# A three-layer kernel with a retention stage: one TensorE visit per retention unit, and the state product taken with a block-diagonal 128x128 operand

## The chip, the cores and the metric

The program runs on one core of one Trainium2 chip. The metric is the device time of one execution in microseconds (us). The core has TensorE (PE in the profile; PEld is its weight load), VectorE (DVE), ScalarE (ACT), GpSimd (POOL) and SyncE (SP), which here issues the DMAs. Each of them works through its own list of instructions in order.

## The reference, cut to what matters

```python
scores = scale * q @ k.T                       # 8 batches, 8 heads, 576 positions, 64 features, all float32
rel = pos[:, None] - pos[None, :]
Dmat = np.where(rel >= 0, gamma[head] ** rel, 0.0)
att = (scores * Dmat) @ v                      # retention
x = att, heads side by side                    # 4608 tokens x 512
h = x @ w_in;  y = (h * cos(h)) @ w_out        # 512 -> 2048 -> 512
z = max(y @ w1, y @ w2, y @ w3) @ w_out2       # 512 -> 768 -> 512
```

gamma is one constant below 1 for each head. The three dense layers make up most of the work; the change touches only the retention, the second to fourth lines.

## The kernel before, in words

The 4608 tokens are cut into 9 blocks of 512 columns, and the 8 heads into 4 pairs. One block of one head pair is a **unit**: 36 units, numbered block by block, and a unit holds both heads of its pair, one in partitions 0 to 63 and the other in 64 to 127. A block is cut into 4 chunks of 128 tokens, or 5 where a batch ends inside a chunk and two chunks have only 64. Along each batch the retention is computed chunk by chunk: within a chunk from scores, across chunks through a 64x64 state for each head (the sum of key-value products so far).

For one unit the functions are:

- `att_load` (L555): one DMA of 1 MB brings queries, keys, values and factors into a buffer `u` from an eight-deep pool, which also holds four weight tiles and one tile of background work.
- `att_scale` (L570): POOL multiplies the values by factors that undo the decay (units 3 to 7 on ACT), L578.
- `att_scores` (L584): PE multiplies keys by queries. Each head uses half of the array's rows (64x128), eight float32 matmuls per unit, each recorded as two instructions; the two heads run side by side (L600). Two PSUM banks.
- `att_mask` (L602): DVE masks the scores into the buffer (L609).
- `att_products` (L621): PE multiplies keys by values of a chunk. Each head uses half of the array's columns (128x64), L631. One PSUM bank.
- `att_states` (L635): ACT copies these products into the buffer (L642), POOL adds them up from chunk to chunk (L653); the last chunk's sum goes to `carry`, where the next block of the same heads finds it.
- `att_out` (L658): PE multiplies masked scores by values (**inner** from here on, 128x64, L667), and then queries by states (**outer** from here on, one matmul for each head and chunk in one quarter of the array, 64x64, L679), into one bank.
- `att_decay` (L683): DVE applies the decay and writes the result to the operand of the first dense layer (L695).

The dense product of the first layer runs at the same time on PE. It uses a seven-product scheme (P_A11 to P_A22) on high and low parts of the operands, with matmuls on the whole array (128x128 weights, L422). One product is 12 instructions. The unit of the order is the **slot**, one such product, its copy out of PSUM and then `tick()` (L160), which issues what the agenda holds for that slot. `at(n, fn, turn)` (L149) puts work on the agenda; `AHEAD` work comes first in the slot, `LATER` work last, in the order of its registration. A block has 14 slots (two groups of seven). After a lead-in of 17 slots with units 0 to 7, unit n starts at slot `3 + 11 * (n - 8) // 3`, so the units stand 3, 4 and 4 slots apart. Relative to a unit's start its load is issued at -4, the scaling at -1, the scores at 0, the mask at +1; at +5 a second visit of PE (`att_visit`, L704) computes the next unit's products and this unit's inner and outer, and the next unit's states are issued; at +6 comes the decay.

The operands x of the dense product are built on DVE, ACT and POOL beside this: differences (L391, on POOL for blocks 1 to 7), high parts on ACT (L395), low parts on DVE (L399). A gate (cosine) on ACT and DVE, and the splitting of weights for later layers (totals on POOL, L203), run in the same slots. After the ninth block the first layer goes on without retention, and the other two layers follow.

Of the kernel before, what the change touches and what calls it, by code (L numbers as in the profile page):

```python
# [62 lines left out]
CM = CG + NPAIR * HB  # L66
CM2 = CM + CH
CGS = CM2 + CH
NCONST = CGS + NPAIR * 9
NTV = 8  # L70


def constants():
    gamma = (1.0 - 2.0 ** (-5.0 - np.arange(H, dtype=np.float32))).astype(np.float64)
    c = np.zeros((128, NCONST), np.float64)
    p = np.arange(128)
    for hp in range(NPAIR):
        g = gamma[2 * hp + p // 64]
        c[:, CG + hp * HB : CG + (hp + 1) * HB] = g[:, None] ** np.arange(HB) / math.sqrt(D) / WSCALE
        c[:, CGS + hp * 9 : CGS + (hp + 1) * 9] = g[:, None] ** (64 * np.arange(9))  # L80
    c[:, CM : CM + CH] = np.arange(CH)[None, :] >= p[:, None]
    c[:, CM2 : CM2 + CH] = c[:, CM : CM + CH] * ((np.arange(CH) // 64)[None, :] == (p // 64)[:, None])
    return c.astype(np.float32)
# [23 lines left out]
def retention_ffn(ctx: ExitStack, tc: tile.TileContext, att, w_in, w_out, w123, w_out2, cst, out):  # L107
    nc = tc.nc
# [18 lines left out]
    def f32(t):  # L127
        return t.bitcast(F32)
# [111 lines left out]
    spare = cpool.tile([128, NB], U32, name="spare")  # L240
# [311 lines left out]
    def order_of(n):  # L552
        return divmod(n, NPAIR)

    def att_load(n):  # L555
        j, hp = order_of(n)
        w = w14(f"u{j}_{hp}", F32)
        units[n] = {
            "qk": w[:, : 2 * NB].rearrange("p (a n) -> p a n", a=2),
            "kv": w[:, 2 * NB : 4 * NB].rearrange("p (a n) -> p a n", a=2),  # L560
            "tv": w[:, 4 * NB : 4 * NB + NTV],
            "ret": w[:, 4 * NB + NTV : 6 * NB + NTV].rearrange("p (a n) -> p a n", a=2),
            "sums": w[:, 6 * NB + NTV : 6 * NB + NTV + 4 * D].rearrange("p (k n) -> p k n", n=D),
            "w": w,
        }
        nc.sync.dma_start(out=w[:, : 4 * NB + NTV], in_=att[j, hp])
# [54 lines left out]
    def att_products(n):  # L621

        u = units[n]
        ch = chunks_of(order_of(n)[0])
        kn, v = u["kv"][:, 0], u["kv"][:, 1]
        u["kv_sums"] = b = bank(f"kv{n}")
        for k, i in enumerate(grown(n)):
            s = ch[i][2] // CH
            for e in range(2):
                cols = slice(s * CH + 64 * e, s * CH + 64 * e + 64)  # L630
                nc.tensor.matmul(  # L631
                    b[64 * e : 64 * e + 64, k * D : (k + 1) * D], kn[:, cols], v[:, cols], start=True, stop=True
                )

    def att_states(n):  # L635

        u = units[n]
        j, hp = order_of(n)
        ch = chunks_of(j)
        of = grown(n)  # L640
        su = u["sums"]
        nc.scalar.copy(su[:, : len(of)], u["kv_sums"][:, : len(of) * D].rearrange("p (k n) -> p k n", n=D))  # L642
        before = carry[hp][(j + 1) % 2]
        u["state"] = {}
        for i, (_, m, _, pos) in enumerate(ch):
            if pos:
                u["state"][i] = before
            if i not in of:
                continue
            k = of.index(i)  # L650
            dst = carry[hp][j % 2] if i == len(ch) - 1 else su[:, k]
            if pos:
                nc.gpsimd.tensor_tensor(out=dst, in0=before, in1=su[:, k], op=ALU.add)  # L653
            elif i == len(ch) - 1:
                nc.gpsimd.tensor_copy(dst, su[:, k])
            before = dst

    def att_out(n):  # L658
        u = units[n]
        j, hp = order_of(n)  # L660
        ch = chunks_of(j)
        qT, v = u["qk"][:, 0], u["kv"][:, 1]
        po = u["po"] = bank(f"po{n}")
        for i, (a, m, c, _) in enumerate(ch):
            s = c // CH
            for e in range(2):
                nc.tensor.matmul(  # L667
                    po[64 * e : 64 * e + 64, a : a + m],
                    v[:, s * CH + 64 * e : s * CH + 64 * e + 64],
                    u["ret"][:, e, c : c + m],  # L670
                    start=i == 0,
                    stop=False,
                    skip_group_check=True,
                )
        for i, st in u["state"].items():
            a, m, _, _ = ch[i]
            for e in range(2):
                r = slice(64 * e, 64 * e + 64)
                nc.tensor.matmul(  # L679
                    po[r, a : a + m], st[r], qT[r, a : a + m], start=False, stop=True, skip_group_check=True  # L680
                )

    def att_decay(n):  # L683
# [19 lines left out]

    def att_visit(n):  # L704

        if n + 1 < NUNIT:
            att_products(n + 1)
        att_out(n)

    def att_unit(n, start):  # L710

        if n not in (NLEAD, NLEAD + 1):
            at(max(0, start - 1), lambda: att_scale(n))
        at(start, lambda: att_scores(n), AHEAD)
        at(start + 1, lambda: att_mask(n))
        if not n:
            at(start + 1, lambda: att_products(n), AHEAD)
            at(start + 1, lambda: att_states(n))
        at(start + 5, lambda: att_visit(n), AHEAD)
        if n + 1 < NUNIT:  # L720
            at(start + 5, lambda: att_states(n + 1))
        at(start + 6, lambda: att_decay(n))

    NUNIT = NBLK * NPAIR


    carry = [[f32(spare)[:, (2 * hp + k) * D : (2 * hp + k + 1) * D] for k in range(2)] for hp in range(NPAIR)]
    sums_bank = bank("sums")

    def claim():  # L730
# [83 lines left out]
    at(3, claim)  # L814
    at(4, lambda: lead_in(1, 0, nc.vector, nc.vector, SECOND))
    for n in range(NLEAD):
        att_unit(n, 2 * n + 1)
# [823 lines left out]
```

## Time and profile before

| | |
|---|---|
| median of 3 runs | 1397.0 us (1395.46 to 1397.63) |
| the profiled execution | 1396.51 us, span of its instructions 1394.7 us |
| mean granted TensorE clock | 0.997 |
| PE busy | 1363.3 us (98%) |
| DVE busy | 1129.4 us (81%) |
| ACT busy | 799.0 us (57%) |
| POOL busy | 230.0 us (16%) |
| HBM read, written | 194.28 MB, 137.89 MB |

A busy PE is not PE at its peak: matmuls overlap, and their ends are modelled. To see what work on PE costs, take the time from the start of one group of matmuls to the start of the next in the timeline. "Idle" and "waited" rows name what ended a wait. The retention runs from 8 to 313 us, the lead-in from 0 to some 60 us of it.

### The profile page before, as it was taken

How to read it: one execution, taken by the hardware profiler on the slowest of the kernel's cores; microseconds unless marked ns; L12 is line 12 of the kernel's file. 1: busy time of each engine (PE TensorE's matmuls, PEld its weight loads, DVE VectorE, ACT ScalarE, POOL GpSimd, SP SyncE). 2: the span in 40 equal slices, each digit the busy share in tenths (PEclk: the TensorE clock that was granted, in tenths of full speed). 3: DMA queues.
4: the chain of work that ended last, by engine and by line, in shares of the span. 5: the costliest groups of instructions: out<-in, count | busy, mean ns of one | idle time of the engine just before them, and what ended most of it. 6: DMA issues, size and time to landing. Idle time of an engine off the chain costs nothing.

```text
span 1394.7 us, 22899 instructions
## 1 busy us (share of the span) xinstructions
PE 1363.3 (98%) x8794; PEld 1175.4 (84%) x8794; DVE 1129.4 (81%) x1471; ACT 799.0 (57%) x1238; POOL 230.0 (16%) x259
## 2 busy tenths in 40 slices
PE   7899999999999999999999999999999999999998
PEld 5799999998888887888988888889878888888887
DVE  8988878989687789989879989577777567868884
ACT  6565565568677876666456556444544434444553
POOL 4455555730110000000011110100100000000000
PEclk9999999999999999999999999999999999999999
DMA  9679899988999975664577997343434476255633
GB/s 387 249 286 333 332 343 311 340 314 318 357 349 339 358 286 211 242 226 173 178 258 207 309 255 209 100 154 114 174 134 159 166 273 252 88 180 155 224 106 121
DMA packets 113085, 333.67 MB, mean 239 GB/s; under 512 B 9936, under 2 KB 18256, under 8 KB 107344
## 3 DMA queue, kind: packets, MB, share of 16 engines
q1 hardware_dynamic: 110096, 322.77, 63.9%
q0 software_dynamic: 2880, 9.44, 3.7%
q8 instruction: 69, 1.13, 0.3%
q14 instruction: 40, 0.33, 0.1%
HBM read 194.28 MB, written 137.89 MB: 238 GB/s over the span
## 4 chain that ended last, share of the span: by engine, by line
PE 55%; DMA 5%; DVE 3%; ACT 1%; issue 1%; SPq 0%; ACTq 0%; DVEq 0%
PE d_e L444 12%; PE d_g L976 11%; PE b_g L976 6%; PE b_e L444 6%; PE d_u L1506 5%; PE a_g L976 3%; PE a_e L444 3%; PE b_u L1506 2%; PE d_b L422 2%; PE a_u L1506 1%; DMA mqp<-ext 1%; PE b_b L422 1%; PE d_gs L976 1%; DMA gqp<-s_a 1%; DMA ar_b<-w 1%
## 5 line engine op out<-in xcount | busy, mean ns | idle before, releaser
L976 PE MATMUL d_g<-h_g,w_wo 128*128 128x512 f32 x512 | 157.9, 390 | 0.5 <-ACT o_g L999 0.5
L444 PE MATMUL in<-y,w_wi 128*128 128x512 f32 x672 | 153.0, 389 | 0.0
L444 PEld LDWEIGHTS in<-y,w_wi 128*128 128x128 f32 x672 | 125.9, 188 | 26.5 <-ACT s_a L1112 0.4
L943 DVE TENSOR_TENSOR l_g<-q_g,h_g 128x1024 fp32r<-128x1024 f32 x96 | 116.7, 1229 | 13.9 <-ACT h_g L936 9.5
L469 ACT ACTIVATE ext<-d_e 128x512 f32<-128x512 f32 x72 | 43.1, 599 | 143.1 <-PE d_e L444 143.1
L422 PE MATMUL d_a<-x_x,w_wi 128*128 128x256 f32 x864 | 117.3, 288 | 7.1 <-DVE w_wi L236 4.8
L936 ACT CAST h_g<-q_g 128x1024 fp32r<-128x1024 f32 x96 | 99.0, 1052 | 35.3 <-DVE q_g L927 22.9
L422 PEld LDWEIGHTS d_a<-x_x,w_wi 128*128 128x128 f32 x864 | 107.7, 192 | 12.3 <-DVE w_wi L236 5.0
L976 PEld LDWEIGHTS d_g<-h_g,w_wo 128*128 128x128 f32 x512 | 95.9, 188 | 20.6 <-ACT o_g L999 0.9
L539 DVE SCALAR_TENSOR_TENSOR s_a<-t_a,s_a 128x1024 f32<-128x1024 f32 x68 | 94.1, 1385 | 12.0 <-ACT t_a L536 12.0
L976 PE MATMUL d_g<-l_g,w_wo 128*128 128x512 f32 x256 | 99.8, 390 | 0.2 <-DVE l_g L943 0.2
L530 DVE SCALAR_TENSOR_TENSOR t_a<-s_a,t_a 128x1024 f32<-128x1024 f32 x68 | 88.5, 1303 | 14.2 <-ACT t_a L526 14.2
L526 ACT ACTIVATE t_a<-s_a 128x1024 int32<-128x1024 f32 x68 | 71.9, 1058 | 21.5 <-DVE s_a L1115 15.3
L536 ACT ACTIVATE t_a<-t_a 128x1024 f32<-128x1024 f32 x68 | 72.0, 1059 | 20.5 <-DVE t_a L530 20.2
L444 PE MATMUL d_e<-h_e,w_b 128*128 128x512 f32 x304 | 81.4, 390 | 0.8 <-DVE ext L473 0.8
L976 PE MATMUL b_g<-h_g,w_wo 128*128 128x512 f32 x256 | 79.2, 390 | 1.5 <-ACT h_g L936 1.5
L473 DVE TENSOR_TENSOR ext<-ext,b_e 128x512 f32<-128x512 f32 x36 | 24.7, 686 | 59.4 <-PE b_e L444 51.7
L444 PEld LDWEIGHTS d_e<-h_e,w_b 128*128 128x128 f32 x304 | 56.9, 188 | 12.9 <-DVE ext L473 1.2
L422 PE MATMUL b_a<-x_x,w_wi 128*128 128x256 f32 x432 | 60.6, 290 | 0.9 <-DVE x_x L399 0.9
L976 PEld LDWEIGHTS b_g<-h_g,w_wo 128*128 128x128 f32 x256 | 47.8, 188 | 12.1 <-ACT h_g L936 2.4
L422 PEld LDWEIGHTS b_a<-x_x,w_wi 128*128 128x128 f32 x432 | 55.3, 195 | 3.2 <-DVE x_x L399 1.1
L976 PEld LDWEIGHTS d_g<-l_g,w_wo 128*128 128x128 f32 x256 | 48.1, 188 | 11.0 <-DVE l_g L943 1.0
(371 smaller groups left out, 3322.4 us busy)
## 6 DMA issues: line engine op xcount, KB each, us to landing
u<-att SPq DMA_DIRECT2D x36, 1028.0 KB, 8.3
gqp<-s_a SPq DMA_DIRECT2D x64, 512.0 KB, 6.8
q_g<-gqp SPq DMA_DIRECT2D x64, 512.0 KB, 7.0
xsp<-x_x SPq DMA_DIRECT2D x56, 512.0 KB, 7.5
y<-xsp SPq DMA_DIRECT2D x56, 512.0 KB, 8.8
mqp<-ext SPq DMA_DIRECT2D x24, 512.0 KB, 4.1
st_b<-p_b SPq DMA_DIRECT2D x21, 512.0 KB, 6.4
w_b<-st_b SPq DMA_DIRECT2D x5, 1792.0 KB, 12.8
```

Source lines behind the costliest of these rows:

```text
L422: nc.tensor.matmul(h[:, p * HB : (p + 1) * HB], a, b, start=first and p == 0 and i == 0, stop=i == len(terms) - 1, skip_group_check=True,)
L444: nc.tensor.matmul(dst, a, b, start=first and i == 0, stop=i == len(terms) - 1, skip_group_check=True)
L469: nc.scalar.activation(dst, b[:, :n], AF.Copy, scale=scale)
L473: nc.vector.tensor_tensor(out=dst, in0=dst, in1=b[:, :n], op=ALU.add)
L526: nc.scalar.activation(st["t"], s, AF.Copy, bias=0.25)
L530: nc.vector.scalar_tensor_tensor(out=r, in0=s, scalar=MOST_TURNS, in1=st["t"], op0=ALU.min, op1=ALU.subtract)
L536: nc.scalar.activation(r, r, AF.Sin, scale=TURN, bias=HALF_PI)
L539: nc.vector.scalar_tensor_tensor(out=s, in0=f32(st["t"]), scalar=-1.0, in1=s, op0=ALU.max, op1=ALU.mult)
L936: nc.scalar.copy(h, ts[i][q])
L943: nc.vector.tensor_tensor(out=lo, in0=t, in1=f32(h), op=ALU.subtract)
L976: nc.tensor.matmul(to, a, v[:, p].rearrange("p (b n) -> p b n", b=2) if half and n == 2 else v[:, :, r], start=first and k == 0 and p == 0 ...
L1506: nc.tensor.matmul(dst, a, v, start=first and p == 0 and i == 0 and (wide or mt == 0), stop=p == 2 and i == 2, skip_group_check=True,)
```

## The change

From unit 8 on, a unit has one visit of PE instead of two: at its start the visit computes scores(n), inner(n-1), products(n) and outer(n-1), in this order. What hung on the second visit moves with it: mask and states of unit n, carry and decay of unit n-1 come in the slot after the visit. The last unit's inner and outer get a visit of their own. Loads are issued one slot earlier (-5) and scalings one slot earlier (-2). For units 0 to 7 the slots stay, with the same order inside a visit.

Outer becomes one matmul for each chunk, on the whole array, for the units from 8 on. For this each state is a 128x128 tile with the two heads' 64x64 states on its diagonal and zeros elsewhere. `att_states` makes it with two ACT multiplications by a column of zeros and ones (new constants at CE) in place of one copy; the tiles are laid over the part of the buffer that held the keys for the scores. POOL adds 128x128 tiles instead of 128x64. The carry is also such a tile, one per head pair instead of two that alternate, so its new value is written by a function of its own, `att_carry`, after outer has read the old one. POOL clears it once at the beginning.

```diff
+CE = CGS + NPAIR * 9
+NCONST = CE + 2
...
+            "wide": w[:, NB : 2 * NB].rearrange("p (k n) -> p k n", n=CH),
...
-        su = u["sums"]
-        nc.scalar.copy(su[:, : len(of)], u["kv_sums"][:, : len(of) * D].rearrange("p (k n) -> p k n", n=D))
-        before = carry[hp][(j + 1) % 2]
+        kv = u["kv_sums"][:, : len(of) * D].rearrange("p (k n) -> p k n", n=D)
+        early = n < NLEAD
+        if early:
+            su = u["sums"]
+            nc.scalar.copy(su[:, : len(of)], kv)
+        else:
+            su = u["wide"]
+            for e in range(2):
+                nc.scalar.mul(su[:, : len(of), e * D : e * D + D], kv, cs[:, CE + e : CE + e + 1])
+        held = carry[hp]
+        before, whole = heads(held) if early else [held], None
...
+            t = su[:, of.index(i)]
+            own = rows(t) if early else [t]
+            if i == len(ch) - 1:
+                u["last"] = (heads(held) if early else [held], before if pos else None, own)
+            elif pos and early and whole is not None:
+                nc.gpsimd.tensor_tensor(out=t, in0=whole, in1=t, op=ALU.add)
+            elif pos:
+                for d, a, b in zip(own, before, own):
+                    nc.gpsimd.tensor_tensor(out=d, in0=a, in1=b, op=ALU.add)
+            before, whole = own, t
+
+    def att_carry(n):
...
+        dst, before, own = units[n]["last"]
+        for k, (d, b) in enumerate(zip(dst, own)):
+            if before is None:
+                nc.gpsimd.tensor_copy(d, b)
+            else:
+                nc.gpsimd.tensor_tensor(out=d, in0=before[k], in1=b, op=ALU.add)
...
+    def att_outer(n):
...
         for i, st in u["state"].items():
             a, m, _, _ = ch[i]
-            for e in range(2):
-                r = slice(64 * e, 64 * e + 64)
+            for e, t in enumerate(st):
+                r = slice(0, 128) if len(st) == 1 else slice(64 * e, 64 * e + 64)
                 nc.tensor.matmul(
-                    po[r, a : a + m], st[r], qT[r, a : a + m], start=False, stop=True, skip_group_check=True
+                    po[r, a : a + m], t, qT[r, a : a + m], start=False, stop=True, skip_group_check=True
                 )
...
     def att_visit(n):
 
-        if n + 1 < NUNIT:
-            att_products(n + 1)
-        att_out(n)
+        if n >= NLEAD:
+            att_scores(n)
+        if n:
+            att_inner(n - 1)
+        att_products(n)
+        if n:
+            att_outer(n - 1)
+
+    def att_unit(n, start, visit):
 
         if n not in (NLEAD, NLEAD + 1):
-            at(max(0, start - 1), lambda: att_scale(n))
-        at(start, lambda: att_scores(n), AHEAD)
+            at(max(0, start - (1 if n < NLEAD else 2)), lambda: att_scale(n))
+        if n < NLEAD:
+            at(start, lambda: att_scores(n), AHEAD)
+        at(visit, lambda: att_visit(n), AHEAD)
+        if n:
+            at(visit + 1, lambda: (att_carry(n - 1), att_decay(n - 1)))
         at(start + 1, lambda: att_mask(n))
-        if not n:
-            at(start + 1, lambda: att_products(n), AHEAD)
-            at(start + 1, lambda: att_states(n))
-        at(start + 5, lambda: att_visit(n), AHEAD)
-        if n + 1 < NUNIT:
-            at(start + 5, lambda: att_states(n + 1))
-        at(start + 6, lambda: att_decay(n))
+        at(visit if n < NLEAD else visit + 1, lambda: att_states(n))
...
+    carry = [f32(spare)[:, hp * CH : (hp + 1) * CH] for hp in range(NPAIR)]
+    nc.gpsimd.memset(f32(spare), 0.0)
...
-            at(max(0, start_of(n) - 4), lambda n=n: att_load(n))
-        att_unit(n, start_of(n))
+            at(max(0, start_of(n) - 5), lambda n=n: att_load(n))
+        att_unit(n, start_of(n), start_of(n))
+    at(start_of(NUNIT), lambda: (att_inner(NUNIT - 1), att_outer(NUNIT - 1)), AHEAD)
+    at(start_of(NUNIT) + 1, lambda: att_decay(NUNIT - 1))
```

## Rows read from the trace of the kernel before

**Rows 1.** The page: busy time of the engines, DVE in 40 slices.

```profile
PE 1363.3 (98%) x8794; PEld 1175.4 (84%) x8794; DVE 1129.4 (81%) x1471; ACT 799.0 (57%) x1238; POOL 230.0 (16%) x259
DVE  8988878989687789989879989577777567868884
```

**Rows 2.** Waits of PE, 40:320, then 300:420: total us, times, longest.

```profile
PE d_a L422 <- DVE w_wi L236: 4.8, 1, 4.8
PE d_a L422 <- DVE x_x L399: 1.8, 1, 1.8
...
PE b_a L422 <- DVE x_x L399: 0.9, 1, 0.9
PE d_a L422 <- DVE x_x L399: 0.4, 1, 0.4
```

**Rows 3.** Timeline of PE at unit 20: start us, us, line, instructions.

```profile
163.04 1.16 PE L600 MATMUL sc<-u 64*128 64x128 f32 x16
164.13 1.70 PE L422 MATMUL d_a<-x_x,w_wi 128*128 128x256 f32 x12
165.76 0.69 PE L631 MATMUL kv<-u 128*64 128x64 f32 x16
166.27 1.04 PE L667 MATMUL po<-u 128*64 128x128 f32 x16
167.25 0.43 PE L679 MATMUL po<-u,spare 64*64 64x128 f32 x4
167.52 0.60 PE L679 MATMUL po<-u 64*64 64x128 f32 x8
168.05 1.69 PE L422 MATMUL b_a<-x_x,w_wi 128*128 128x256 f32 x12
169.58 1.60 PE L422 MATMUL sums<-x_x,w_wi 128*128 128x256 f32 x12
```

**Rows 4.** Timeline of PE: unit 35; unit 20's scores until 163.65.

```profile
302.01 0.57 PE L631 MATMUL kv<-u 128*64 128x64 f32 x12
302.41 1.05 PE L667 MATMUL po<-u 128*64 128x128 f32 x16
...
307.38 1.60 PE L422 MATMUL sums<-x_x,w_wi 128*128 128x256 f32 x12
308.82 1.60 PE L422 MATMUL d_a<-x_x,w_wi 128*128 128x256 f32 x12
...
311.37 0.44 PE L679 MATMUL po<-u,spare 64*64 64x128 f32 x4
...
312.39 1.70 PE L422 MATMUL d_a<-x_x,w_wi 128*128 128x256 f32 x12
...
163.04 0.83 PE L600 MATMUL sc<-u 64*128 64x128 f32 x10
```

**Rows 5.** ACT and POOL operations of the states: ns min/median/max; ACT's copy-out.

```profile
L642 ACT COPY u<-kv x36: 304/354/374, 12.4 to 302.6; 128x256 f32<-128x256 f32 x20, 128x192 f32<-128x192 f32 x16
L653 POOL TENSOR_TENSOR u<-u x48: 316/322/1187, 12.8 to 303.8; 128x64 f32<-128x64 f32 x48
L578 POOL TENSOR_TENSOR u<-u x31: 1037/1047/2072, 9.4 to 295.0; 128x512 f32<-128x512 f32 x31
169.78 0.60 ACT L469 ACTIVATE s_a<-b_a 128x512 f32<-128x512 f32 x1 [2.40 <-PE b_a L422]
```

**Rows 6.** Waits of POOL and SP, 40:320; the page's unit loads.

```profile
POOL u L653 <- ACT u L642: 79.9, 25, 6.9
...
SPq L566 <- PE po L679: 47.4, 17, 5.8
...
u<-att SPq DMA_DIRECT2D x36, 1028.0 KB, 8.3
```

**Rows 7.** Windows: length, busy us of PE, PEld, DVE, ACT, POOL; clock, DMA.

```profile
280.00:300.00 20.00, 20.00 (x230) 18.49 (x230) 18.48 (x26) 12.66 (x21) 11.53 (x12) 1.00 0.90 336
...
320.00:340.00 20.00, 18.48 (x147) 17.75 (x147) 19.71 (x32) 17.34 (x28) 0.00 (x0) 1.00 0.97 354
```

More of the change, by code (lines that the diff above doesn't have):

```diff
@@ L68 @@
 CGS = CM2 + CH
-NCONST = CGS + NPAIR * 9
+CE = CGS + NPAIR * 9
+NCONST = CE + 2
 NTV = 8
@@ L80, in constants @@
         c[:, CGS + hp * 9 : CGS + (hp + 1) * 9] = g[:, None] ** (64 * np.arange(9))
+    for e in range(2):
+        c[:, CE + e] = p // 64 == e
     c[:, CM : CM + CH] = np.arange(CH)[None, :] >= p[:, None]
@@ L633, in att_products, with heads, rows @@
                 )
+    def heads(t):
+        return [t[64 * e : 64 * e + 64, 64 * e : 64 * e + 64] for e in range(2)]
+    def rows(t):
+        return [t[64 * e : 64 * e + 64] for e in range(2)]
     def att_states(n):
@@ L640, in att_states @@
         of = grown(n)
-        su = u["sums"]
-        nc.scalar.copy(su[:, : len(of)], u["kv_sums"][:, : len(of) * D].rearrange("p (k n) -> p k n", n=D))
-        before = carry[hp][(j + 1) % 2]
+        kv = u["kv_sums"][:, : len(of) * D].rearrange("p (k n) -> p k n", n=D)
[5 more added lines that the diff above has]
+            su = u["wide"]
+            for e in range(2):
+                nc.scalar.mul(su[:, : len(of), e * D : e * D + D], kv, cs[:, CE + e : CE + e + 1])
+        held = carry[hp]
+        before, whole = heads(held) if early else [held], None
         u["state"] = {}
@@ L649, in att_states, with att_inner @@
                 continue
[L650 to L658, printed above, removed]
+            t = su[:, of.index(i)]
[9 more added lines that the diff above has]
+    def att_carry(n):
+        if "last" not in units[n]:
+            return
+        dst, before, own = units[n]["last"]
[4 more added lines that the diff above has]
+                nc.gpsimd.tensor_tensor(out=d, in0=before[k], in1=b, op=ALU.add)
+    def att_inner(n):
         u = units[n]
-        j, hp = order_of(n)
-        ch = chunks_of(j)
-        qT, v = u["qk"][:, 0], u["kv"][:, 1]
+        ch = chunks_of(order_of(n)[0])
+        v = u["kv"][:, 1]
         po = u["po"] = bank(f"po{n}")
@@ L674, in att_out @@
                 )
+    def att_outer(n):
+        u = units[n]
+        ch = chunks_of(order_of(n)[0])
+        qT, po = u["qk"][:, 0], u["po"]
         for i, st in u["state"].items():
             a, m, _, _ = ch[i]
-            for e in range(2):
-                r = slice(64 * e, 64 * e + 64)
+            for e, t in enumerate(st):
+                r = slice(0, 128) if len(st) == 1 else slice(64 * e, 64 * e + 64)
                 nc.tensor.matmul(
-                    po[r, a : a + m], st[r], qT[r, a : a + m], start=False, stop=True, skip_group_check=True
+                    po[r, a : a + m], t, qT[r, a : a + m], start=False, stop=True, skip_group_check=True
                 )
@@ L704, in att_visit @@
     def att_visit(n):
-        if n + 1 < NUNIT:
-            att_products(n + 1)
-        att_out(n)
-    def att_unit(n, start):
-        if n not in (NLEAD, NLEAD + 1):
-            at(max(0, start - 1), lambda: att_scale(n))
-        at(start, lambda: att_scores(n), AHEAD)
-        at(start + 1, lambda: att_mask(n))
-        if not n:
-            at(start + 1, lambda: att_products(n), AHEAD)
-            at(start + 1, lambda: att_states(n))
-        at(start + 5, lambda: att_visit(n), AHEAD)
-        if n + 1 < NUNIT:
-            at(start + 5, lambda: att_states(n + 1))
-        at(start + 6, lambda: att_decay(n))
+        if n >= NLEAD:
[6 more added lines that the diff above has]
+    def att_unit(n, start, visit):
+        if n not in (NLEAD, NLEAD + 1):
+            at(max(0, start - (1 if n < NLEAD else 2)), lambda: att_scale(n))
[4 more added lines that the diff above has]
+            at(visit + 1, lambda: (att_carry(n - 1), att_decay(n - 1)))
+        at(start + 1, lambda: att_mask(n))
+        at(visit if n < NLEAD else visit + 1, lambda: att_states(n))
     NUNIT = NBLK * NPAIR
-    carry = [[f32(spare)[:, (2 * hp + k) * D : (2 * hp + k + 1) * D] for k in range(2)] for hp in range(NPAIR)]
+    carry = [f32(spare)[:, hp * CH : (hp + 1) * CH] for hp in range(NPAIR)]
+    nc.gpsimd.memset(f32(spare), 0.0)
     sums_bank = bank("sums")
@@ L816, in retention_ffn @@
     for n in range(NLEAD):
-        att_unit(n, 2 * n + 1)
+        att_unit(n, 2 * n + 1, 2 * n + 4 if n else 2)
     at(13, lambda: lead_in(2, 0, nc.vector, nc.vector, SPREAD))
```

## The prediction

> **What bounds the kernel now.** I read the page first: PE is busy for 98% of the span, DVE for 81%, and in the eight slices that hold the retention (the second to the ninth) DVE shows 7 to 9 tenths [rows 1]. Next the waits: the two waits of PE in the first view (4.8 us for a weight, 1.8 for an operand x) end the lead-in, before 67 us; the next two (0.4 and 0.9 us) come behind the retention, at 322 and 326 us [rows 2]. Between them PE waits for nobody. So in these 246 us time is saved only by giving PE less to do, and each microsecond taken from PE counts until another engine is late. Last the timeline of PE around one unit, group by group [rows 3], since a busy share says nothing of what a group costs.
>
> **What a change of tile shape costs.** A product (12 instructions, whole array) that follows and precedes another takes 1.44 us (308.82 - 307.38) [rows 4]. One with retention on one side takes 1.53 (169.58 - 168.05), one with retention on both 1.63 (165.76 - 164.13) [rows 3]. So PE pays .09 to .10 us on the product's side, at the leaving and at the coming back. The other half of each change is in the retention's own groups:
>
> - Scores: six instructions, three pairs, are .33 us (1.16 - .83), so .11 a pair and .88 for eight [rows 3, 4]. They take 1.09: .21 too much, for entry and exit.
> - Key-value products: 16 instructions .51, 12 are .40 [rows 3, 4]; four cost .11, 16 cost .44, so .07 for the entry.
> - Outer: three chunks .80, four .22 more (1.02, 311.37 to 312.39) [rows 3, 4]; so .22 a chunk of 128, and .14 for entry and exit.
> - Inner: .98 for four chunks [rows 3], at .22 each .88; .10 for the exit to outer's shape. Between products and inner (same shape) nothing is lost.
>
> Sum for one unit before: product side .09 + .10 + .09 + .10 = .38, scores .21, products .07, inner .10, outer .14: .90 us.
>
> **The change on PE.** One visit enters scores (.09 + .10), goes to inner's shape (.11 + .07, the entry as in products), runs inner and products in that shape, and leaves it for the whole array (.10, as inner did, and .10 for the late first matmul, as at a product). After outer the next product has the same shape: 0. Sum .57, so .33 less for a unit. Units 9 to 35 make 27 visits: 8.9 us. The last unit's own visit pays .09 + .07 + .10 + .10 = .36 where it paid .09 + .10 + .14 + .10 = .43: .1. Together 9.0 us.
>
> Against that stands the rate of outer. Two heads side by side take .22 for a chunk. Whole-array float32 with 128 columns isn't in the trace; one matmul is again two recorded instructions, each between .11 (a pair of scores, 128 weight columns for each head) and .12 (a product's instruction, 1.44 / 12) [rows 3, 4]. So 0 to .02 for a chunk of 128, of which units 8 to 35 have 80 with a state: 0 to 1.6 us, and I take 0.8, the middle. Chunks of 64 (20) are .11 now by the rate of products; with whole weights two instructions are .11 to .22, so 0 to 2.2 us; I take 0, since a pair of products already loads 2 x 64 weight columns in .055.
>
> The Trainium skill, "TensorE: Matmul & The Clock Gate", section "LDWEIGHTS (loading the stationary operand)", counts 128 weight columns at about 107 ns, whatever the rows. By it the short chunks would cost the upper end, some 2 us by an estimate from that page. The rows don't bear it out: two loads of 64 columns fit in .055.
>
> The boundary from outer (float32) to the product (another float format, same shape) isn't in the trace either. Its bounds are 0 and .20 us (both halves at a change of shape) a unit, 5.4 us in all; I take 0, because between products and inner, the only neighbours of one shape but different work, nothing is lost [rows 3]. The Trainium skill, "TensorEngine Tiling (Array Packing)", "Key Properties", says that changing the tiling mode drains the array, and changing only the tile doesn't; by that it is 0 too, though no row here has a change of format.
>
> **The other engines.** ACT gets a second operation of .35 us per unit [rows 5]: 10 us over 246. It is busy 12.7 of 20 us [rows 7], and the copy that PE needs soonest (the seed of the third product) has one whole product, 1.44 us, as cover; without it, .35 a unit would be 10 us. DVE's work stays; mask and decay come earlier.
>
> POOL is the tight place. Its chain for unit n+1: visit(n), the slot's product, ACT's copy of it (.60), two multiplications (.7), one to three additions, the scaling of n+1, then products(n+1). From the visit's start: scores 1.09, inner .07 + .88, products .44, outer .10 + .10 + .66 are 3.3; product 1.4, copy .6, multiplications .7: 6.1; additions of 128x128, interpolated between 128x64 (.32) and 128x512 (1.05), .42 each: 6.5 to 7.4; scaling 1.05: 7.6 to 8.4 [rows 3 to 5]. With units three slots apart products(n+1) starts at .1 + 3.3 + 3 x 1.44 + 2.0 = 9.8. So 1.4 to 2.2 us remain, 0.4 in the worst case with a disturbed scaling (2.07) [rows 5]; four slots apart it is 1.4 more, less one difference or total in some units. The wait of POOL for ACT, 80 us now [rows 6], shows that POOL has time; the carry's addition goes into it. I take 0.3 us of waits.
>
> SP issues unit loads a slot earlier, ahead of a slot's other DMAs. They wait for the outer of three units before (47 us in 17 waits [rows 6]), which now ends one or two slots earlier, so the place in the queue costs nothing; a load lands in 8.3 us [rows 6] and has some seven slots. POOL's clearing of the carry, one 128x512 operation (at most 2 us [rows 5]), lies in the first microseconds of the lead-in, whose end is set by DVE: 0, bounds -1 to +1.
>
> What is late next is DVE. Between visits PE now runs three or four products in a row instead of one or two, while DVE's work per slot stays; and from 280 us DVE is busy 18.5 of 20 us, and 19.7 from 320 us [rows 7]. PE waits there already, 1.3 us in two waits [rows 2]. Five visits less their .33 are 1.7 us that DVE, with 1.5 us idle in 20, can follow only in part: I take 1.0 us more of waits behind the retention, and 0.9, one wait of the longest such size [rows 2], in the block that has no visit between its first and third product (the seventh). Bounds 0 and 4.
>
> Sum: 9.0 - 0.8 - 0.3 - 1.9 = 6.0 us less. The later stages shift as a whole. The profiled execution took 1396.5 us (span 1394.7), half a microsecond below the median of the runs: 1390.5 for the changed kernel, against either within their spread of 2 us.
>
> **The rivals.**
>
> - **Operands late (DVE):** each of eight blocks has a wait of 0.5 us, half the longest seen, and the tail 2: 6 us instead of 1.9, so 1394.6. For it speaks DVE's 92%; against it that before, with DVE at the same work, no block had one.
> - **The format boundary costs like a shape boundary:** 5.4 us go back: 1395.9. For it: PE never had this neighbourhood. Then the change doesn't do what it says: the full-array product would save nothing.
> - **POOL turns it round:** with disturbed additions (1.2 each, two or three) and scaling (2.07), the chain ends at 10.6 to 11.8, not 9.8. Nine three-slot units would lose 1.4 each, half of the other 18 some 0.5: 17 us, against 6.3 gained: 1407. It decides from .23 us lost per visit on. Against it: the medians (.32, 1.05) stand near the minima [rows 5].
> - **Nothing late:** the existing 1.3 us of waits go as well, as the last decay comes two slots earlier, and outer keeps its rate: 1396.5 - 9.0 - 1.3 = 1386.2.
>
> **How the numbers follow.** Forecast 0.52 (own range 1388 to 1392.5), DVE 0.17, boundary 0.10, POOL 0.09, nothing late 0.12. 0.2% is 2.8 us, about what a measurement here can tell from no change: faster means below 1393.9. To it go the forecast, nothing late, and almost half of the DVE case and a little of the boundary (its waits may be shorter): 0.75. Same: the rest of these two, and a fifth of POOL: 0.17. Slower 0.08. For 8 in 10 the range goes from 1385.5 to 1395.5: it leaves out POOL and the upper half of the boundary.
>
> **What would show it.** PE's timeline: scores, inner, products, outer directly behind each other; outer of three chunks in .66 to .72 plus .1, the following product in 1.44 or 1.53, not 1.63. PE in the retention ends some 8 us earlier. If waits of PE name POOL's scaling (L578's successor) or the states, POOL is the rival that holds; if they name the low parts of x in many blocks, DVE. A product behind outer at 1.63 shows the boundary. The prediction is wrong if the span from the first visit to the last shrinks by less than 5 us, or if what is won there is waited for before 345 us.

## The result, and the profile after

| | before | after |
|---|---|---|
| median (4 runs each, same chip) | 1397.32 us (1395.46 to 1397.82) | 1410.01 us (1407.42 to 1414.27) |
| profiled execution, span | 1396.51, 1394.7 us | 1408.14, 1406.3 us |
| mean granted TensorE clock | 0.997 | 0.991 |

The changed kernel takes 1.0093 times as long, 95% interval 1.0066 to 1.012: 12.7 us slower, where 6 us faster was forecast. The prediction was wrong in its sign.

The page's line of busy times, after, and below it the clock's line in 40 slices; the first answers to [rows 1]:

```profile
PE 1363.7 (97%) x8594; PEld 1183.6 (84%) x8594; DVE 1145.1 (81%) x1471; ACT 808.0 (57%) x1266; POOL 250.6 (18%) x268
...
PEclk9899999999999999999999999999999999999999
```

PE has 200 instructions less (its matmuls on pairs of heads became single ones). DVE has the same 1471 instructions and is 15.7 us longer busy with them: the same work became slower. These sums don't say where the time went. The waits of PE do; kernel after, 100 to 340 us (total us, times, longest):

```profile
PE d_a L425 <- DVE x_x L402: 9.1, 5, 3.4
PE sums L425 <- DVE x_x L402: 2.6, 2, 1.6
PE sc L604 <- DVE k_x L730: 1.0, 1, 1.0
PE b_a L425 <- DVE x_x L402: 0.8, 1, 0.8
```

In [rows 2] PE waits for nobody in this stretch until 322 us. Now it waits 13.5 us for DVE, nearly all of it for x_x, the low parts of the dense product's operands (L402 is the L399 of before).

To put the waits and PE's own work apart, I took the time from the start of each dense product (products and blocks are counted from 0) to the start of the next, and for each step the smallest over all kernels of one kind that ran (two visits, or one visit with the full-array outer). Between product 12 and product 113 these smallest steps add up to 241.4 us with two visits and to 235.8 with the change: undisturbed, PE would gain 5.6 us here. The profiled executions took 242.0 and 254.6. So before lost 0.5 us to waits and the like, after lost 18.8. The whole difference of the two profiled executions is 1.1 us by product 12, 12.6 from there to product 113, 0.9 to product 125, and 3.0 given back in the later stages.

The timeline of PE, after: two visits that nobody disturbs, the one around the longest wait, and an outer of four whole chunks (start us, us, line, instructions; idle time before it and its releaser in brackets):

```profile
100.44 1.16 PE L604 MATMUL sc<-u 64*128 64x128 f32 x16
...
103.03 0.49 PE L714 MATMUL po<-u,spare 128*128 128x128 f32 x2
103.36 0.78 PE L714 MATMUL po<-u 128*128 128x64 f32 x6
103.95 1.68 PE L425 MATMUL sums<-x_x,w_wi 128*128 128x256 f32 x12
...
136.53 1.60 PE L425 MATMUL sums<-x_x,w_wi 128*128 128x256 f32 x12
138.06 1.16 PE L604 MATMUL sc<-u 64*128 64x128 f32 x16
139.15 1.09 PE L697 MATMUL po<-u 128*64 128x128 f32 x16
140.07 0.52 PE L635 MATMUL kv<-u 128*64 128x64 f32 x12
140.52 0.49 PE L714 MATMUL po<-u,spare 128*128 128x128 f32 x2
140.85 0.61 PE L714 MATMUL po<-u 128*128 128x128 f32 x4
141.21 0.96 PE L425 MATMUL d_a<-x_x,w_wi 128*128 128x256 f32 x6
...
190.83 0.64 PE L425 MATMUL d_a<-x_x,w_wi 128*128 128x256 f32 x4
194.90 2.08 PE L425 MATMUL d_a<-x_x,w_wi 128*128 128x256 f32 x8 [3.43 <-DVE x_x L402]
196.91 2.08 PE L604 MATMUL sc<-u 64*128 64x128 f32 x16
...
201.97 1.68 PE L425 MATMUL d_a<-x_x,w_wi 128*128 128x256 f32 x12
...
295.59 0.49 PE L714 MATMUL po<-u,spare 128*128 128x128 f32 x2
...
296.50 1.68 PE L425 MATMUL b_a<-x_x,w_wi 128*128 128x256 f32 x12
```

The visit at 138 us takes 3.15 us (141.21 - 138.06), and its parts are those of the forecast. The visit at 196.91 takes 5.06 us for what took 3.51 at 100.44. The windows around it show why (length, busy us of PE, PEld, DVE, ACT and POOL; granted clock, DMA share, GB/s):

```profile
190.00:193.50 3.50, 1.47 (x13) 1.27 (x11) 3.50 (x7) 3.47 (x7) 3.34 (x4) 0.99 0.90 207
193.50:200.30 6.80, 5.40 (x40) 4.95 (x42) 3.69 (x4) 1.54 (x2) 0.94 (x2) 0.50 0.87 293
200.30:220.00 19.70, 19.70 (x230) 18.95 (x227) 17.09 (x26) 10.73 (x18) 10.53 (x11) 1.00 0.89 297
```

PE stood for 3.43 us until 194.90. The granted clock fell to 0.50, that is from the level of 2.4 GHz to that of 1.2, at 193.5 and came back at 200.3. A second such stretch of 3.4 us begins at 234.5, behind a wait of 2.4 us; behind the wait of 2.7 us that ends at 273.15 the clock stayed up. The kernel before has no half clock between 67 us and its end.

Between products 12 and 113 (78.8 to 333.4 us) after has seven waits, 12.0 us in sum. The two products with the half clock took 6.06 and 3.65 us more than their smallest steps, which is 3.9 more than their waits of 3.43 and 2.38; the other five took 1.5 more than their waits. That is 17.4 of the 18.8 us lost; the rest is in delays too short for a line in the view of waits.

Why DVE was late at that wait, for the operand of the fourth product of block 4, is seen in its timeline, after:

```profile
183.46 3.07 DVE L200 SCALAR_TENSOR_TENSOR ar_wi<-ar_wi 128x512 uint32<-128x512 uint32 x1
186.45 1.21 DVE L533 SCALAR_TENSOR_TENSOR t_a<-s_a,t_a 128x1024 f32<-128x1024 f32 x1
...
189.95 1.40 DVE L613 TENSOR_TENSOR u<-sc,cs 128x384 f32<-128x384 f32 x4
191.27 2.13 DVE L542 SCALAR_TENSOR_TENSOR s_a<-t_a,s_a 128x1024 f32<-128x1024 f32 x1
193.32 1.52 DVE L402 TENSOR_TENSOR x_x<-tb_x,x_x 128x512 fp32r<-128x512 f32 x1
```

The same place in DVE's timeline of the kernel before:

```profile
181.62 0.69 DVE L197 SCALAR_TENSOR_TENSOR ar_wi<-ar_wi 128x512 uint32<-128x512 uint32 x1
...
186.15 1.34 DVE L539 SCALAR_TENSOR_TENSOR s_a<-t_a,s_a 128x1024 f32<-128x1024 f32 x1
...
188.32 0.88 DVE L399 TENSOR_TENSOR x_x<-tb_x,x_x 128x512 fp32r<-128x512 f32 x1
```

PE's timeline before, there (the product at 188.67 is the one that uses this operand):

```profile
184.88 0.44 PE L679 MATMUL po<-u,spare 64*64 64x128 f32 x4
...
185.69 1.70 PE L422 MATMUL b_a<-x_x,w_wi 128*128 128x256 f32 x12
...
188.67 1.79 PE L422 MATMUL d_a<-x_x,w_wi 128*128 128x256 f32 x12
190.40 1.16 PE L600 MATMUL sc<-u 64*128 64x128 f32 x16
```

And POOL's timeline, after, in that stretch:

```profile
183.47 1.27 POOL L394 TENSOR_TENSOR tb_x<-k_x,ta_x 128x512 f32<-128x512 f32 x1
184.71 1.27 POOL L394 TENSOR_TENSOR ta_x<-k_x,k_x 128x512 f32<-128x512 f32 x1
...
191.04 1.27 POOL L394 TENSOR_TENSOR tb_x<-tb_x,k_x 128x512 f32<-128x512 f32 x1
192.27 2.02 POOL L582 TENSOR_TENSOR u<-u 128x512 f32<-128x512 f32 x1
```

The same three DVE operations take 3.07, 2.13 and 1.52 us after, 0.69, 1.34 and 0.88 before: 3.8 us more. Beside the first, POOL runs two differences back to back; beside the last two, a difference and a scaling. Between products 12 and 113, what DVE's operations take above their undisturbed durations (about the shortest that each kind of operation took; the **excess** from here on) adds up to 26.1 us before and 39.1 after.

The Trainium skill, "SBUF — State Buffer", section "🔬 SBUF: two separate sides", says that DVE and GpSimd share one pair of ports under an exclusive lock: an operation of DVE with two operands in SBUF and one of GpSimd that reads SBUF don't run side by side, and the later one waits for the whole of the other. By it the first operation would take 0.69 + 2 x 1.27 = 3.2 us as an estimate; the row has 3.07. That agrees for this operation, though the two rows start 0.01 us apart and don't tell which came first. POOL's two differences were not held up: 1.27 us is about the shortest that they take (1.26 before). Its scaling beside DVE's last two operations was: 2.02 us, against 1.05 at the median in [rows 5].

ACT waits longer for DVE as well; the first line of its waits between 67 and 315 us, after:

```profile
ACT t_a L539 <- DVE t_a L533: 42.8, 17, 5.8
```

The line that answers to it, before:

```profile
ACT t_a L536 <- DVE t_a L530: 19.7, 10, 4.5
```

ACT waits twice as long for the gate's DVE step. That its copies and high parts then reach DVE and POOL late is argued and not shown: POOL's waits for ACT's copies of the state products fell, from 77.5 to 36.3 us in the same stretch.

### The profile page after: what moved, and what is told of

Same layout as the page of the kernel before. It is cut to its first block, busy times and chain, and to the rows that moved or that the text cites. A ratio compares the mean times of both kernels' runs of the same rounds, so it can differ in the third digit from the quotient of the medians.

```text
span 1406.3 us, 22495 instructions
## 1 busy us (share of the span) xinstructions
PE 1363.7 (97%) x8594; PEld 1183.6 (84%) x8594; DVE 1145.1 (81%) x1471; ACT 808.0 (57%) x1266; POOL 250.6 (18%) x268
## 4 chain that ended last, share of the span: by engine, by line
PE 66%; DVE 5%; DMA 4%; ACT 2%; issue 1%; SPq 0%; POOL 0%; ACTq 0%; DVEq 0%
PE d_e L447 13%; PE d_g L1016 11%; PE in L447 9%; PE b_e L447 6%; PE b_g L1016 6%; PE d_u L1546 5%; PE a_g L1016 3%; PE a_e L447 3%; PE b_u L1546 2%; PE d_b L425 2%; PE a_u L1546 1%; PE b_b L425 1%; DMA gqp<-s_a 1%; DMA ar_b<-w 1%; PE d_gs L1016 1%
## 5 line engine op out<-in xcount | busy, mean ns | idle before, releaser
L425 PEld LDWEIGHTS d_a<-x_x,w_wi 128*128 128x128 f32 x864 | 109.5, 196 | 16.5 <-DVE x_x L402 12.6
L533 DVE SCALAR_TENSOR_TENSOR t_a<-s_a,t_a 128x1024 f32<-128x1024 f32 x68 | 90.5, 1332 | 12.6 <-ACT t_a L529 12.6
L604 PE MATMUL sc<-u 64*128 64x128 f32 x576 | 46.4, 304 | 12.9 <-DMA u<-att 11.9
```

Of the source, the lines that this page charges most:

```text
L425: nc.tensor.matmul(h[:, p * HB : (p + 1) * HB], a, b, start=first and p == 0 and i == 0, stop=i == len(terms) - 1, skip_group_check=True,)
L533: nc.vector.scalar_tensor_tensor(out=r, in0=s, scalar=MOST_TURNS, in1=st["t"], op0=ALU.min, op1=ALU.subtract)
L604: nc.tensor.matmul(u["sc"][e][:, sl], u["qk"][r, 1, sl], q, start=True, stop=True)
```

## The experiments

Two theories stood at first. **A**: the merged visit is what makes the operands late, since it holds back the other engines' work for 3.2 to 3.7 us and then gives it to them in a pile, with three or four products in a row. **B**: the wider states are, through the work that they add on POOL and ACT. The expectations that follow are the texts written before the runs; all ratios are to the kernel before, run beside each on the same chip, with 95% intervals.

**visit_only**: one visit, states 64 wide and one matmul for each head, as before. The carry stays one tile per head pair, so POOL adds a unit's first sum and its carry head by head, in two additions of 64x64 where before has one of 128x64.

```diff
-        early = n < NLEAD
+        early = True
```

> One visit per unit, states and outer as before (64-wide states, a matmul for each head). Theory A (the merged visit: with three or four products in a row DVE's low parts are due sooner than it can bring them, PE waits and its clock falls) expects the loss to stay: 1403 to 1411 us, waits of PE for low parts over 8 us before 340 us. Theory B (POOL's additions on 128x128 tiles hold up DVE) expects it gone: 1389 to 1396, waits under 4 us.

1407.56 us, ratio 1.0081 (1.006 to 1.0103). PE's waits, 70 to 345 us:

```profile
PE d_a L425 <- DVE x_x L402: 6.2, 4, 2.7
PE b_a L425 <- DVE x_x L402: 2.1, 3, 0.9
PE sums L425 <- DVE x_x L402: 1.6, 2, 0.8
```

The merged visit without the wider tiles brings 10 of the 12.7 us, and the same waits, as A expected. It doesn't part the visit from POOL's work, though: POOL is busier here than in either kernel (160.0 us between 77 and 320 us, against 131.3 before and 149.4 after). DVE's excess is some 35 us. Undisturbed, its products 12 to 113 take 238.6 us: merging alone saves PE 2.8 of the 5.6.

**states_only**: the two visits of before, with the wider states and the full-array outer.

```diff
-        if n >= NLEAD:
-            att_scores(n)
...
+        if n + 1 < NUNIT:
+            att_products(n + 1)
+        att_inner(n)
+        att_outer(n)
...
+        at(start + 6, lambda: (att_carry(n), att_decay(n)))
```

> Two visits as before, states as 128x128 tiles with the whole-array outer. Theory A expects 1394 to 1399 us, with no wait of PE for low parts between 70 and 320 us. Theory B expects 1403 to 1411 us, with PE waiting for low parts, and DVE's and POOL's instructions longer, as in the changed kernel.

1402.62 us, 1.0052 (1.0036 to 1.0068). Its largest wait of PE:

```profile
PE d_a L425 <- DVE x_x L402: 3.6, 5, 1.3
```

A expected no loss here, and missed: the wider states alone cost 5 us, with the same operand late in five blocks (in one of them, block 8, by 0.4 us as before). Neither theory alone explains this and visit_only.

**pool_extra**: before, with a second POOL addition of about 128x120 behind each state addition from unit 8 on.

```diff
                 nc.gpsimd.tensor_tensor(out=dst, in0=before, in1=su[:, k], op=ALU.add)
+                if n >= NLEAD:
+                    nc.gpsimd.tensor_tensor(out=..., in0=..., in1=..., op=ALU.add)
```

> The kernel before with a second POOL addition (128x120, a result that nobody reads) behind each addition of states from unit 8 on, some 25 us more of POOL. Theory A expects 1395 to 1399 us, as POOL has idle time. Theory B expects 1402 to 1411: DVE's instructions beside it get longer and PE waits for low parts.

1396.33 us, 0.9998 (0.998 to 1.0017). POOL was 42 us longer busy (272.2 us) and DVE's excess rose by 6 us to 32.1, as in states_only, and the time didn't move beyond its interval. The trace still has two new waits, 0.5 and 0.3 us, at the fourth products of blocks 4 and 5:

```profile
PE d_a L422 <- DVE x_x L399: 1.3, 3, 0.5
```

So B falls as it stood: more POOL work isn't enough; it matters where it lands.

**pieces_early**: after, with the high parts of a block's later operands one or two slots earlier (the low parts follow each high part).

```diff
-        build_in(..., (-11, -4, -3, -1), (-10, -8, -3, -1, 1, 1, 4), ...)
+        build_in(..., (-11, -4, -3, -1), (-10, -8, -4, -3, -1, -1, 2), ...)
```

> The changed kernel with the high and low parts of the third to seventh operand of each block issued one or two slots earlier. Theory A (they are due too soon after being issued) expects most of the waits of PE to go, with the clock at full speed from 80 us on: 1387 to 1396 us. Theory B (DVE has too much to do) expects the waits to stay within a third: 1401 to 1410.

1401.43 us, 1.0025 (1.0011 to 1.0039). 8.6 of 12.7 us come back, and the low parts are gone from PE's waits. Others have come up:

```profile
PE sums L425 <- ACT sums L495: 3.4, 4, 1.0
PE kv L635 <- POOL u L582: 2.3, 4, 0.9
```

The time lies at the edge of B's range, but the waits for low parts, which B expected to stay, are gone: the low parts' due time was most of it, and behind them stand ACT's seeds and POOL's scaling. DVE's excess is 40.6 us, no smaller than in after.

**one_piece**: after, with the fourth operand alone two slots earlier.

```diff
-        build_in(..., (-10, -8, -3, -1, 1, 1, 4), ...)
+        build_in(..., (-10, -8, -3, -3, 1, 1, 4), ...)
```

> The changed kernel with only the fourth operand (P_S2) of blocks 1 to 8 built two slots earlier. If that one operand's due time is the place where the gain is lost (theory A, narrow), the waits of PE for low parts before the fourth product go in all blocks, with the two clock drops near 193 and 234 us: 1393 to 1399 us. If late operands are only where a general lack of DVE time shows (theory C: DVE, with its waits for ACT, has no time left in a block at the new pace), the waits come back at other operands: 1402 to 1409.

1401.25 us, 1.0019 (0.9999 to 1.004), between the two ranges: 8.8 us back by moving one operand, as much as by moving five. What is left:

```profile
PE b_a L425 <- DVE x_x L402: 5.5, 3, 2.2
PE sums L425 <- DVE x_x L402: 2.5, 2, 1.6
```

The d_a wait of 9.1 us is gone; the operands behind it are late now, by 8.0 us in sum, but in waits that are shorter: 2.2 us at most instead of 3.4. The two clock drops are gone; one of 3.4 us has come at 127.6 us, behind a wait of 1.6.

**visit_pieces**: visit_only with the earlier operands of pieces_early (both edits are shown above).

> One visit per unit with the states as before, and the third to seventh operand built one or two slots earlier. ACT and POOL have less to do than in the changed kernel with the same operands early (1401.4). Theory A: the visit's saving on PE (.27 us for each of 27 units by the timeline) shows at last: 1388 to 1394 us. Theory C: 1397 to 1404.

1399.88 us, 1.0016 (1.0002 to 1.003). A's number missed, that of C was met. Two premises of the expectation fail: POOL has more to do here, not less (161.4 us between 77 and 320 us, 151.9 in pieces_early), and the merging saves PE 2.8 us over 25 visits, .11 each and not .27. Products 12 to 113 lose 5.6 us where visit_only lost 14.4; the largest wait is POOL's scaling:

```profile
PE kv L635 <- POOL u L582: 2.7, 2, 1.9
```

**before_pieces**: the kernel before with the earlier operands, as a control (same edit).

> The kernel before with the same operands one or two slots earlier, as the control of the two kernels that have them early. It has 1.3 us of waits behind the retention and about 0.5 us inside to lose: 1394 to 1397 us by theory A. By theory C no change, 1396 to 1399.

1394.55 us, 0.9976 (0.9964 to 0.9989), 10 runs, as A expected. The two waits behind the retention in [rows 2] are gone (one of 0.7 us for a seed of ACT's has come there), and it is the fastest complete kernel that ran: it beats both, the kernel before by 3.4 us (1397.96 beside it) and the changed one by 15.5, on medians from two chips. Beside the retention it gains nothing (products 12 to 113 take 242.0 us in both): in the profiled executions 1.3 us of the gain lie behind it, before product 125, and 1.8 in the later stages. What the earlier operands are worth depends on the kernel: 3.4 us here, 8.6 with the merged visit.

**visit_split**: after, with the merged visit cut in two: scores and inner in their slot, products and outer one slot later, with decay, carry and states a slot later as well.

```diff
+        def rest():
+            att_products(n)
+            if n:
+                att_outer(n - 1)
...
+        if n > NLEAD:
+            at(1, rest, AHEAD)
...
```

> The changed kernel with each visit cut in two: scores and inner at its slot, products and outer one slot later, with carry, decay and states one slot later too. This costs PE two more changes of shape, .4 to .5 us a unit, 12 us in all, against the changed kernel. If the length of one visit is what makes ACT and DVE late (their queues stand 4 to 5 us at the copy of a product behind it), the waits for low parts fall under 5 us and the clock drops go: 1398 to 1404 us in spite of the cost. If not, the waits stay and the cost adds: 1412 to 1422.

1408.16 us, 1.0081 (1.0054 to 1.0107), between the two ranges: inconclusive. The low parts still cost 5.4 us of waits, and a seed 2.4 in one. The fourth operand was relieved in part, from 9.1 us to 4.0, and one clock drop of two went:

```profile
PE d_a L425 <- DVE x_x L402: 4.0, 4, 1.9
```

**after_no_join and before_no_join**: without the second step (join, L199 and L200) in seven conversions of later weights that run on DVE beside the retention. This takes DVE's longest single delay away.

```diff
-                lambda: join(st[raw], st["t"]),
+                lambda: None if skip else join(st[raw], st["t"]),
...
+        at(per * j + 1, lambda: background(*back.pop(0), True, 3, skip=True))
```

> The changed kernel without the two DVE operations that join the halves of a weight (L199, L200), in the seven background conversions that run beside the retention: 28 operations, 15 us of DVE by their undisturbed times; the weights of later layers come out wrong. If DVE's time is what the new pace lacks (theory C), most of the loss goes and the saving on PE shows: 1388 to 1397 us. If only the place in the order of the low parts counts (theory A, narrow), 1401 to 1409, since the joins stand in other slots than the fourth operand's low part.

> The kernel before without the same 28 DVE operations, as control. PE waits there for 1.3 us only, behind the last of them, so both theories expect 1394.5 to 1398 us.

After: 1403.31 us, 1.0033 (1.0019 to 1.0047), 6.7 us back, in the range of the narrow theory A. Before: 1397.6, 1.0002 (0.9987 to 1.0017), nothing. The same DVE work costs 6.7 us in one kernel and nothing in the other: before, DVE had room for the join. The low parts are still waited for in after (7.8 us), so the join is a part of the cause and not the whole.

**pieces_no_join**: both, the earlier operands and no join.

> The changed kernel with the third to seventh operand early and without the same 28 DVE operations. Theory C: what was still lost with early operands (1401.4) was DVE's time, so the whole saving shows: 1385 to 1391 us. If instead ACT or POOL is what holds now (the seeds on ACT, the scalings on POOL), 1394 to 1401.

1396.94 us, 0.9995 (0.9976 to 1.0015): 13.1 us back, all that the change had lost, and yet not the gain on PE, which C expected. The largest waits now:

```profile
PE kv L635 <- POOL u L582: 3.0, 5, 0.8
PE sums L425 <- ACT sums L495: 1.6, 2, 1.0
```

Products 12 to 113 lose 7.0 us still. No wait is longer than 1 us, and the clock never falls beside the retention. With DVE relieved, POOL and ACT are the next in line.

**after_no_scale**: after without POOL's scaling from unit 10 on. It was to show how much of DVE's lateness is POOL's largest operation.

```diff
+            if n < NLEAD + 2:
                 nc.gpsimd.tensor_tensor(out=v, in0=v, in1=..., op=ALU.mult)
```

> The changed kernel without POOL's scaling of the values from unit 10 on (26 operations, 1.05 to 2.07 us each; the result comes out wrong). Theory D: POOL's work now comes in one dense run behind ACT's multiplications, and DVE's instructions beside it are held up (those beside the retention are 39 us longer than undisturbed, 26 before); then DVE's excess falls under 30 us, the waits of PE for low parts under 6 us, and the time to 1396 to 1402. Theory C (DVE's queue and its coupling with ACT and PE, whatever POOL does): 1405 to 1410.

1402.47 us, 1.0035 (1.0024 to 1.0047), 7.5 us back, just over the range of D. DVE's excess fell from 39.1 to 28.1 us, near before's 26.1, as D expected. But PE waits on, 9.4 us for low parts where D expected under 6; the largest of it:

```profile
PE d_a L425 <- DVE x_x L402: 6.6, 4, 3.0
```

So even with DVE's operations nearly as short as before, the fourth operand is late: the order in which the merged visit releases the work counts beside the collisions.

**decay_late**: after, with the decays of units 8 to 34 one slot later, out of the pile behind the visit.

```diff
-            at(visit + 1, lambda: (att_carry(n - 1), att_decay(n - 1)))
+            at(visit + 1, lambda: att_carry(n - 1))
+            at(visit + (2 if n > NLEAD else 1), lambda: att_decay(n - 1))
```

> The changed kernel with the decays of units 8 to 34 one slot later, so that mask and decay no longer stand together in DVE's queue in the slot behind a visit. If that pile is what makes the low parts late: 1400 to 1405. If not (theories C and D): 1407 to 1412, as what DVE must do before the low part of the fourth operand stays.

1404.19 us, 1.0054 (1.0032 to 1.0076), within the range for the pile: 5.8 us back, though its interval and that of after overlap. The wait moved in part onto the decay, for which the key-value products wait now:

```profile
PE d_a L425 <- DVE x_x L402: 6.0, 4, 2.6
...
PE kv L635 <- DVE k_x L730: 1.6, 2, 1.4
```

**Taken together.** Each relief of DVE gives back a part: a later due time 8.8 us, no scaling 7.5, no join 6.7, a later decay 5.8. These are differences of medians from different chips, and the interval of after alone is some 4 us to either side, so their order isn't shown. They overlap (due times and joins together 13.1), so no single one is the cause. What they have in common is the operand that had no margin. Shown: that a merged visit without the wider tiles brings most of the loss, that its waits are for low parts of x, that moving one of them takes back two thirds, and that POOL's added work by itself costs nothing clear of the noise in the old order. Open: how the loss of visit_only divides over the visit and POOL's smaller additions; how the remaining part divides over ACT, DVE and POOL; the 1.1 us lost in the lead-in; why the later stages give back 3.0 us. The price of the half clock (up to 3.9 us) is read from the traces, and no run took it away by itself.

## Why the prediction was wrong, step by step

- **The step that failed is "What is late next is DVE".** It named the right engine and, in "three or four products in a row", what sets it under pressure, and mis-sized it: 1.9 us of waits with bounds of 0 and 4, against 13.0 us more of waits (14.4 between 70 and 345 us, 1.4 before), and up to 3.9 of half clock behind them that no term had. Behind the retention its size was right (1.0 us more). The other 12.0 us stand in blocks 2 to 7, where it had 0.9 in one block, and for a reason that doesn't hold: the seventh block, counted from 0 or from 1, does have a visit between its first and third product (steps of 4.9 and 5.0 us), and it is blocks 3 and 4 that have none. Three errors lie in it. First, the margin: "between them PE waits for nobody" was read as room. At the place that counts there was none. In the rows of before shown above, the low part that starts at 188.32 ends at 189.20; the product that needs it started at 188.67, and it took 1.73 us to the next group (190.40) where 1.53 is usual. That is a delay of 0.2 us, too small for a line of its own in a view of waits. Second, its due time, which the prediction doesn't reckon: the low part of the fourth operand is issued behind the second product of a block, and the fourth product needs it. From the start of the second product to that of the fourth the smallest steps are 3.0, 5.3 and 5.5 us before in blocks 4, 5 and 6, and 2.9, 3.0 and 3.0 after: in blocks 5 and 6 a visit stood between them and stands there no more. The waits of 3.4, 2.4 and 2.7 us lie just there; in blocks 3 and 7, where these two steps take 6.1 and 6.4 us after, the fourth product waits 0.2 us at most. In block 4 the time was as short before; there DVE, held up beside POOL, comes late: without POOL's scaling that wait is 0.8 us (after_no_scale, at 188.7), while blocks 5 and 6 keep 2.4 and 3.0. Third, "DVE's work stays" counted operations and not their durations: the same 1471 took 15.7 us more.
- **The rival "Operands late (DVE)"** was the mechanism, with 0.17; its price of 0.5 us a block came from the longest wait seen, 0.9, and DVE late by one disturbed operation is late by 2.4 us already (3.07 - 0.69). Its objection ("before, with DVE at the same work, no block had one") is the same misreading of a zero margin.
- **The shape changes** were nearly right. In a unit of full chunks the products and the retention between them took 2.62 + 3.80 + 1.53 = 7.95 us before (steps from product to product) and take 4.68 + 1.52 + 1.44 = 7.64 now: 0.31 saved, where the forecast's 0.33 less the measured rate of three chunks (.05) gives 0.28.
- **The rate of outer** was too low. A full chunk takes 2 x .1115 us after and 2 x .1025 before: .018 more, 1.4 us over 80 chunks, where I took 0.8. A short chunk takes as long as a full one after: from outer's start to the next product four chunks take .92 us with two short ones (103.03 to 103.95) and .91 with none (295.59 to 296.50). Before, four chunks take 1.02 with none short [rows 4] and .81 with two (184.88 to 185.69). So a short chunk takes .22 after and some .10 before: .12 more, 2.4 us over 20, where I took 0, with bounds of 0 and 2.2. In the trace after, weight loads of 128 columns begin .11 us apart, for short chunks as for full ones. The Trainium skill, "TensorE: Matmul & The Clock Gate", section "LDWEIGHTS (loading the stationary operand)", had it right with about 107 ns for 128 columns, and my reading of the rows against it was wrong. In the trace before, the two loads of 64 columns that fit in .055 start .006 us apart, in two tiles: they lie side by side, and their time is no rate of columns. Within products 12 to 113 lie 25 of the 27 visits; forecast for them were 7.6 us, of which 0.6 and 2.4 go here; the shape changes give some 0.8 more (25 x .03), and 5.6 were measured.
- **The format boundary** costs nothing, as taken. The product behind outer shows 1.51 to 1.52 us, not 1.44, but its first matmul starts .03 us behind outer's last instead of .11, and its next one .20 later instead of .12: .23 either way. So the rival "format boundary" falls, and the sign that I named for it (the length of that product alone) would have misled.
- **POOL:** PE waits for its scaling nowhere between 100 and 340 us, so the rival "POOL turns it round" falls as it was told. POOL's part is another: it lengthens DVE's operations, and it is next in line once DVE is relieved.
- **The sum:** PE's part was forecast at 8.2 over 27 visits (7.6 over the 25 between products 12 and 113), and 5.6 were measured over these; waits were forecast at 2.2, and 13.0 more of waits and up to 3.9 of half clock were found.

## What to carry to other kernels

An engine without waits may still have no margin: before moving work on a full engine, measure for each operand how long before its use it is ready (a step that is 0.2 us too long is the sign), not whether the view of waits has a line. Merging visits takes a few tenths of a microsecond from PE at each, and it also takes work out from between the issue of an operand and its use; move the due times of the operands built beside it first, which here was worth 3.4 us without the merging and 8.6 with it. A microsecond of waiting on PE cost some 1.4 here ((12.0 + 3.9 + 1.5) / 12.0), since the product with the wait loses a little more than the wait and the clock fell behind two of them.

## What the runs showed of the hardware

- The granted clock fell from 2.4 to 1.2 GHz in the course of a single wait of 3.4 us, at 193.5 us, and stayed there for 6.8 us. Behind waits of 2.4 us (after, 234.5 us) and 1.7 us (pieces_early, 122.7 us) it fell for 3.4 us. The length of the wait alone doesn't decide it: behind 2.7 us (after, 273.15 us) it stayed up. In pieces_no_join, with no wait above 1 us beside the retention, it didn't fall there.
- One DVE operation of 128x512 took 3.07 us beside two POOL operations of 1.27 us, and 0.69 without.
- Adding 42 us of POOL work to a kernel whose DVE is 88% busy between products 12 and 113 left its time within the noise (pool_extra).
- Between whole-array matmuls of different float formats PE loses nothing (.23 us over two instructions on either side of it); between array shapes it loses some .2.
- Four float32 matmuls on the whole array took .91 to .92 us to the start of the next product, whether all had 128 moving columns or two of them 64; weight loads of 128 columns begin .11 us apart.
